# Running the feed-forward part for three groups per block in place of two

## Chip, cores, metric

The kernel runs on one core of a Trainium2 chip. The metric is the device time of one execution in microseconds, lower is better. "Clock" below is the TensorE clock that was granted, as a share of full speed. Times in running text that have no run named are from the instruction times of the profiled execution.

## The reference

For each of 8 batches: squared-relu attention without a softmax, gated by u; then, over all tokens, a feed-forward layer whose hidden unit is the larger of two products.

```python
# u, v: (8, 3072, 256)   z: (8, 3072, 64)
scores = (1/S) * z @ z.T                 # symmetric
attn   = maximum(scores, 0) ** 2
x      = u * (attn @ v)                  # (24576, 256)
g      = maximum(x @ w1, x @ w2)         # d_ff = 1024
out    = g @ w_out                       # fp32
```

## The kernel before

A *group* is 512 query rows: 6 groups a batch, 48 in all, numbered i; g is the number within the batch. A group's attention is 48 *steps* (24 key tiles n, two halves dc of d_model), each a pair of matmuls with 64 rows that run side by side on the two halves of the array.

As the scores are symmetric, a block of scores is made once, by the group that comes first, and turned by DMA transposes on the SyncE queue for the later one. A block *on* the diagonal is its own mirror: in batches 1 to 7 the upper triangle alone is made, and the rest comes from three transposes in place.

```python
def score_pair(b, g, m, ...):            # one pair of score matmuls, relu, square
    ...
    triangle = blk == g and whole_first < (b, g)
    ...                                  # PE: s_ps; ACT: relu -> r_sb; DVE: r*r -> a_sb
    if triangle and m % 2 == 1:
        for j in range(G - 1):
            nc.sync.dma_start_transpose(a[:, j + 1 :, ts(j, P)], a[:, j, (j + 1) * P :])
    if m % 2 == 1 and blk > g:
        if b == 0 and g < 2 and blk > 2:
            later.append((b, g, blk))    # mirrored some steps later
        else:
            mirror(b, g, blk)            # nc.sync.dma_start_transpose -> at_sb
```

`tiles_of` puts the group's own (diagonal) tiles last, n = 20 to 23. Score pairs are made up to 11 ahead of need, at the steps that `pair_slots` lists. Two groups' x wait until a *block*: ff1 (x times w1 - w2, relu) and ff2 (times w_out, plus x times w2 w_out), 128 rows, about 7.8 us of TensorE per group.

```python
def ff_follows(i):
    return i >= 2 and i % 2 == 0 or i == len(groups) - 1
def edge(i):                             # how many last steps are skewed: dc 0 first, then dc 1
    return 0 if ff_follows(i) else 4 if i < 2 else 9
...
for i, (b, g) in enumerate(groups):
    for slot, (n, dc) in enumerate(steps_of(i)):
        ...                              # score pairs, attention step, drain, gate, loads
        if i + 1 < len(groups):
            if i and n == 1:  load_u(*groups[i + 1])     # POOL queue
            if n == 16:       turn_u(*groups[i + 1])     # SyncE queue, transpose
        ...
        if g >= 3 and n in (8, 14) and not late:         # next batch's v, POOL queue
            load_v(b + 1, V_ORDER[2 * (g - 3) + (n == 14)] * G, G)
    now = waiting if ff_follows(i) else []
    g_sbs = [ff(w) for w in now[:1]]
    sums = new or drain(acc, range(KD))
    for j, w in enumerate(now):
        if j: g_sbs.append(ff(w))
        ff2(*w, g_sbs[j])                # o_ps -> ACT copy -> o_sb (2 buffers) -> SyncE queue -> out
```

## Time and profile before

Median 968.79 us (968.57 to 969.14).

| | before |
|---|---|
| span of the profiled execution | 966.4 us |
| TensorE busy, granted clock | 99%, 1.00 |
| DVE, ACT busy | 50%, 58% |
| attention of a group, batches 1 to 7 (first to last attention matmul) | 10.2 to 12.0 us |
| two groups' block with its two ends | 16.3 us |

From the page (busy us and share of the span; the clock's line has 40 equal slices, 9 is 90% or more):

```profile
span 966.4 us, 19478 instructions
...
PE 954.8 (99%) x7994; PEld 621.6 (64%) x8042; DVE 487.2 (50%) x847; ACT 557.6 (58%) x1058; POOL 61.0 (6%) x118
...
PEclk9999999999999999999999999999999999999999
DMA  9999798988689976999869988699967998767611
...
```

There is no slack to see on TensorE. Two small waits of the weight loads (us in total, times, longest) mark a block's ends. They are idle time of the loads; the matmuls themselves start about 0.2 us later per block (0.092 and 0.010 us at the first two of ff1, 0.096 us behind ff2):

```profile
...
PEld L234 <- issue: 9.8, 23, 0.4
...
PEld L147 <- issue: 4.6, 22, 0.2
...
```

### The profile page before, as it was taken

The page shows a single profiled execution, that of the slowest core. Times are in us where ns is not written, and L with a number is a line of the kernel's source. Part 1 is how long each engine was busy: PE and PEld are TensorE (multiplying, and loading weights), DVE is VectorE, ACT ScalarE, POOL GpSimd, SP SyncE. Part 2 cuts the span into 40 slices and gives each one's busy share as a digit, 9 for nine tenths or more (in the row PEclk, how much of TensorE's full clock was granted, in tenths as well). Part 3 has the DMA queues.
Part 4 walks back from the last instruction along what each step waited for, and adds up shares of the span by engine and source line. Part 5 has one row for each costly group of instructions (what it writes and reads, how often), then busy time and mean ns, then how long its engine had stood idle before and what let it go on. Part 6 is the DMA issues. An engine that isn't in the chain of part 4 may idle for free.

```text
span 966.4 us, 19478 instructions
## 1 busy us (share of the span) xinstructions
PE 954.8 (99%) x7994; PEld 621.6 (64%) x8042; DVE 487.2 (50%) x847; ACT 557.6 (58%) x1058; POOL 61.0 (6%) x118
## 2 busy tenths in 40 slices
PE   8999999999999999999999999999999999999998
PEld 4465667675666756667566765676756776566655
DVE  6746454463555534555346553464545554445433
ACT  6757466563575645756456564565556656466433
POOL 3001000100000000000000000000000000000000
PEclk9999999999999999999999999999999999999999
DMA  9999798988689976999869988699967998767611
GB/s 186 186 207 175 135 156 158 179 149 166 134 140 188 146 157 126 164 185 148 150 133 146 184 152 160 131 162 176 150 141 140 157 170 168 135 131 145 124 56 44
DMA packets 382296, 145.99 MB, mean 151 GB/s; under 512 B 360832, under 2 KB 361984, under 8 KB 382208
## 3 DMA queue, kind: packets, MB, share of 16 engines
q1 hardware_dynamic: 365792, 115.25, 62.5%
q0 software_dynamic: 16416, 29.50, 20.8%
q8 instruction: 63, 1.03, 0.4%
q14 instruction: 25, 0.20, 0.1%
HBM read 59.77 MB, written 25.17 MB: 88 GB/s over the span
## 4 chain that ended last, share of the span: by engine, by line
PE 96%; DVE 1%; issue 1%; ACT 1%; DMA 1%; DVEq 0%; POOLq 0%
PE o_ps L263 17%; PE d_ps L234 17%; PE s_ps L147 7%; PE o_ps L255 4%; DMA v_sb<-in_v_dram 1%; DVE a_sb L166 1%; PE acc_12604 L199 1%; PE acc_6354 L199 1%; PE acc_4771 L199 1%; PE acc_3187 L199 1%; PE acc_11103 L199 1%; PE acc_9519 L199 1%; PE acc_7936 L199 1%; PE acc_1582 L199 1%; PE acc_1581 L199 1%
## 5 line engine op out<-in xcount | busy, mean ns | idle before, releaser
L199 PEld LDWEIGHTS <-v_sb 64*128 64x128 bf16 x4608 | 314.6, 94 | 181.4 <-issue 5.9
L160 ACT ACTIVATE r_sb<-s_ps 128x512 bf16<-128x512 f32 (+3 forms) x664 | 333.8, 555 | 90.4 <-PE s_ps L147 88.8
L166 DVE TENSOR_TENSOR a_sb<-r_sb 128x1024 bf16<-128x1024 bf16 x251 | 173.6, 692 | 243.0 <-ACT r_sb L160 239.0
L244 DVE TENSOR_SCALAR g_sb<-d_ps 128x512 bf16<-128x512 f32 x192 | 132.8, 692 | 146.1 <-PE d_ps L234 146.1
L263 PE MATMUL o_ps<-w_out_sb,g_sb 128*128 128x256 bf16 x1536 | 199.1, 273 | 0.0
L234 PE MATMUL d_ps<-xT,w_sb 128*128 128x512 bf16 x720 | 167.4, 379 | 2.6 <-issue 0.2
L263 PEld LDWEIGHTS <-g_sb 128*128 128x128 bf16 x1536 | 150.2, 98 | 20.8
L242 ACT ACTIVATE g_sb<-d_ps 128x512 bf16<-128x512 f32 x192 | 114.8, 598 | 82.0 <-PE d_ps L234 57.1
L147 PE MATMUL s_ps<-zT 64*128 64x512 bf16 (+3 forms) x672 | 148.6, 357 | 0.9 <-DVE r_sb L158 0.5
L270 ACT COPY o_sb<-o_ps 128x512 f32<-128x512 f32 x96 | 56.3, 586 | 150.3 <-PE o_ps L263 149.2
L234 PEld LDWEIGHTS <-w_sb 128*128 128x128 bf16 x768 | 73.2, 98 | 89.6 <-issue 9.8
L255 PE MATMUL o_ps<-W2o_sb,xT 128*128 128x256 bf16 x384 | 73.3, 273 | 0.0
L118 POOL DMA_DIRECT2D un<-in_u_dram x48 | 25.7, 537 | 731.2 <-DMA uT<-un 717.6
L147 PEld LDWEIGHTS <-zT 64*128 64x128 bf16 x672 | 47.6, 94 | 29.0 <-issue 4.6
L220 DVE SCALAR_TENSOR_TENSOR xT<-h_sb,uT 128x512 bf16<-128x512 f32 x96 | 61.8, 685 | 0.0
L164 DVE TENSOR_TENSOR a_sb<-r_sb 128x512 bf16<-128x512 bf16 (+3 forms) x170 | 47.9, 323 | 14.7 <-ACT r_sb L160 14.5
L255 PEld LDWEIGHTS <-xT 128*128 128x128 bf16 x384 | 37.6, 98 | 14.1
L114 POOL DMA_DIRECT2D v_sb<-in_v_dram x48 | 25.8, 546 | 59.1 <-DVE v_sb L113 58.3
L199 PE MATMUL acc_134<-a_sb,v_sb 64*128 64x512 bf16 x24 | 8.7, 377 | 0.5 <-DMA v_sb<-in_v_dram 0.4
L199 PE MATMUL acc_136<-a_sb,v_sb 64*128 64x512 bf16 x24 | 8.7, 378 | 0.0
L199 PE MATMUL acc_137<-a_sb,v_sb 64*128 64x512 bf16 x24 | 8.5, 376 | 0.0
L199 PE MATMUL acc_135<-a_sb,v_sb 64*128 64x512 bf16 x24 | 8.5, 376 | 0.0
(577 smaller groups left out, 1665.3 us busy)
## 6 DMA issues: line engine op xcount, KB each, us to landing
out_dram<-o_sb SPq DMA_DIRECT2D x47, 512.0 KB, 4.0
v_sb<-in_v_dram POOLq DMA_DIRECT2D x48, 256.0 KB, 7.0
un<-in_u_dram POOLq DMA_DIRECT2D x48, 256.0 KB, 5.0
zn<-in_z_dram POOLq DMA_DIRECT2D x7, 384.0 KB, 6.7
a_sb<-a_sb SPq DMA_TRANSPOSE x126, 2.7
at_sb<-a_sb SPq DMA_TRANSPOSE x120, 5.0
uT<-un SPq DMA_TRANSPOSE x48, 3.3
w_132<-in_moe_w_dram POOLq DMA_DIRECT2D x1, 512.0 KB, 5.1
```

The costliest lines, as they stand in the source:

```text
L147: nc.tensor.matmul(s_ps[h][:, lo[h] :], zT[b][rows, 2 * m + h, :], zT[b][rows, g * G + lo[h] // P : g * G + G, :].rearrange("p t c -> p (t ...
L160: nc.scalar.activation(o, s, AF.Relu)
L164: nc.vector.tensor_mul(a[:, k + h, lo[h] :], o, o)
L166: nc.vector.tensor_mul(a[:, k : k + 2, :], r, r)
L199: nc.tensor.matmul(o, v_sb[b][rows, t, ts(dc, P)], mv, start=first, stop=last)
L220: nc.vector.scalar_tensor_tensor(out=xT[:, dc, :].rearrange("p (t r) -> p t r", r=P), in0=hs[dc].rearrange("p (t r) -> p t r", r=P), scala ...
L234: nc.tensor.matmul(d_ps, w15_sb[:, kc, ts(nb, P)], xT[:, kc, :], start=(kc == 0), stop=(kc == KD - 1),)
L242: nc.scalar.activation(g_sb[:, nb, :], d_ps, AF.Relu)
L244: nc.vector.tensor_single_scalar(out=g_sb[:, nb, :], in_=d_ps, scalar=0.0, op=ALU.max)
L255: nc.tensor.matmul(o_ps[:, t, :], xT[:, dc, ts(t0 + t, P)], W2o_sb[:, dc, :], start=(dc == 0), stop=False,)
L263: nc.tensor.matmul(o_ps[:, t, :], g_sb[:, nb, ts(t0 + t, P)], w_out_sb[:, nb, :], start=False, stop=(nb == KF - 1),)
L270: nc.scalar.copy(o_sb[:, t0 : t0 + 2, :], o_ps)
```

## The change

The intent is to switch TensorE between attention and feed-forward less often: 16 blocks in the loop in place of 24. The rest of the diff moves the startup conditions along (the first block is behind group 3) and adapts the score slots.

```diff
     def ff_follows(i):
-        return i >= 2 and i % 2 == 0 or i == len(groups) - 1
+        return i >= 3 and i % 3 == 0 or i == len(groups) - 1
     def edge(i):
-        return 0 if ff_follows(i) else 4 if i < 2 else 9
+        return 0 if ff_follows(i) else 4 if i < 3 else 9
@@ pair_slots
+        if i % 3 == 2:
+            return [3, 9, 14, 19, 24, 29, 41]
@@ main loop
-                    if i < 2:
+                    if i < 3:
                         new[dc] = drain_fast(acc, dc)
-                if i in (1, 2) and n == 10:
+                if i in (1, 2, 3) and n == 10:
-                if i == 2 and n == 16:            # w1 - w2, turn of w2
+                if i == 3 and n == 16:
-            if i == 2:                            # w2 w_out
+            if i == 3:
```

## The prediction

> **What bounds the kernel now.** TensorE. The page has PE busy 954.8 of 966.4 us, clock granted 1.00; in the chain of waits PE holds 96%. In the instruction times, pairs of 64-row matmuls start every 0.216 us, the 512-column d_ps matmuls every 0.216, the 256-column o_ps ones every 0.109. Behind 55 us almost nothing is lost between them except at the ends of an ff block. VectorE is busy 50%, ScalarE 58%. In the first 55 us PE waits for a_sb several times (0.4 to 0.7 us each), as score pairs are needed soon after they are made.
>
> **What a block costs.** Going from attention (64-row tiles) to ff1 (128 rows) the start-to-start distance is 0.09 to 0.11 us above the matmul's own time (up to 0.20 where one row half runs ahead, which is not a cost of the switch), one more 0.01 follows, and from ff2 back to scores it is 0.096 above. The table of waits agrees: PE's weight loads idle before ff1 23 times, before scores 22 times. The Trainium skill, "TensorEngine Tiling (Array Packing)", Key Properties, says that changing the tiling mode drains TensorE; here that is about one exposed weight load (94 to 98 ns) each way, so about 0.205 us per block.
>
> **What the change does.** Ff blocks inside the loop go from 24 to 16 (behind groups 3, 6, ... 45 and 47); no work goes away. Eight blocks fewer: 8 x 0.205 = -1.6 us, all on the critical path. Group 2 of each later batch had its last score pair at slot 26, whose multiply queued behind the two gate operations (2 x 0.685 us on VectorE); the first user waited about 0.09 us. The new slot 24 puts the multiply ahead of the gate: lead 2.37 us against an unqueued latency of 2.36 us (score start to product ready). At most -0.6 us over 7 batches, or nothing. Ends of groups without a block keep the nine-step skew, which shows no wait: 0.
>
> **What it costs.** In group 2 of the first batch the new slots (3, 9, 14, 19, 24, 29, 41) put the last score pair one unit ahead of its first user: lead 0.43 us, latency 2.36, so a PE wait of about 1.9 us near 49 us. The wait of 0.54 us that stood at 50.3 us goes (w2's turn on PE moves to group 3, where leads are 3.4 us or more). The boundary of groups 2 and 3 with four steps of skew: +0.1. The z of the next batch is loaded at group 2, n = 20 (landing took 6.8 us) and doubled on VectorE at group 3, n = 4; a block lay between, now about 5 us: VectorE may wait, mostly hidden by leads: +0.2. Mirrored block (2,3) landed at 54.2, is needed at about 56: no wait. Sum: about +1.7 us.
>
> **Predicted:** -1.6 -0.4 +1.7 gives -0.3; as slots are evidently placed with care, I lean lower: 968.1 us, 8 times in 10 between 966.4 and 970.0. Faster by over 2%: 0.005; within 2%: 0.985; slower: 0.01.
>
> **What would show it.** Right: 16 idle gaps before the first weight load of ff1, not 24, each as long as before; one PE wait for a_sb of 1.7 to 2.2 us at the end of group 2; clock 1.00; busy times of DVE and ACT equal within 1%. Wrong: new PE waits recurring once per batch at the end of group 2 (slot 24 too tight) or group 5, or PE waiting for at_sb transposes or for zd near 55 to 60 us.
>
> **What would make it wrong.** A zn landing later than 58 us, or a transpose queue backing up in groups 2 and 3, whose 16 us of ff cover is gone: +1 to +4 us.

## More of the kernel before

Batch 1, group 2 ends its attention at 172.4 us, the block of two groups lies between, group 3 runs from 188.6 to 200.2 us (start, duration of the issue, line, operation):

```profile
...
164.59 13.59 SPq L181 DMA_TRANSPOSE at_sb<-a_sb  x3
178.27 1.55 SPq L122 DMA_TRANSPOSE uT<-un  x1
179.93 3.76 SPq L169 DMA_TRANSPOSE a_sb<-a_sb  x3
183.79 5.67 SPq L274 DMA_DIRECT2D out_dram<-o_sb  x2
190.84 3.54 SPq L181 DMA_TRANSPOSE at_sb<-a_sb  x1
...
```

The diagonal of group 3 (the three of line 169) is issued at 179.9 to 183.7, and the last of the three lands at 189.4. TensorE asks for the last of them at step n = 23, about 198 us (nine steps and one score pair before the end of the group). It is nearly 9 us early; without the 16.3 us of the block it would be 7 to 8 us late.

## The result

Median 1016.83 us (1013.88 to 1025.83), against 968.79: the ratio is 1.051 (95% interval 1.046 to 1.056). A ratio is the mean time of one kernel's runs over that of the other's of the same rounds, so not quite the ratio of the medians. Executions over 1.5% slower than the fastest of the same kernel are left out of the means. The predicted range ended at 970.0. All five runs have a granted clock of 0.975 to 0.983, where the kernel before has 1.00, and they differ by 1.2%, where those before differ by 0.1%.

```profile
span 1013.7 us, 19464 instructions
...
PE 968.4 (96%) x7994; PEld 630.3 (62%) x8042; DVE 489.7 (48%) x849; ACT 558.2 (55%) x1058; POOL 60.9 (6%) x118
...
PEclk9999999799998999999999899998999999999999
DMA  9996989978679676896848969489794987849611
...
```

The busy time of ACT and DVE is the same to 1% (558.2 and 489.7 us); TensorE has idle slices and slices with a lowered clock, at regular distances. First to last attention matmul of each group tells where (us):

| group in the batch | before, batches 1-7 | after, batches 1 to 7 |
|---|---|---|
| 2 | 11.97 each | 11.55, then 11.65 each |
| 3 | 11.55 each | 19.23, 18.92, 16.20, 18.22, 16.56, 15.55, **11.90** |
| 4 | 11.81 each, last 10.41 | 11.49 each, last 10.30 |
| from the end of group 3 to group 4 (block) | (no block) | 26.57, 25.99, 25.35, 25.72, 26.73, 25.74, **24.05** |
| from the end of group 0 to group 1 (block) | 16.28 each | 24.10 each |

Only group 3 and the block behind it are long, in batches 1 to 6. Batch 7, which has the same instructions but no next batch to load, is not. TensorE at the end of group 3 of batch 1 (start, us, engine, line; in brackets the idle time and what ended it):

```profile
...
186.96 0.38 PE L199 MATMUL acc_2472<-a_sb,v_sb 64*128 64x512 bf16 x1
189.24 0.37 PE L199 MATMUL acc_2471<-a_sb,v_sb 64*128 64x512 bf16 x1 [1.90 <-DMA a_sb<-a_sb]
...
190.50 0.48 PE L199 MATMUL acc_2471<-a_sb,v_sb 64*128 64x512 bf16 x1 [0.66 <-DMA a_sb<-a_sb]
...
195.30 0.58 PE L199 MATMUL acc_2471<-a_sb,v_sb 64*128 64x512 bf16 x1 [3.85 <-DMA a_sb<-a_sb]
...
196.27 0.61 PE L234 MATMUL d_ps<-xT,w_sb 128*128 128x512 bf16 x1
197.10 3.19 PE L234 MATMUL d_ps<-xT,w_sb 128*128 128x512 bf16 x7 [0.22 <-issue]
```

Three waits, each for one of the in-place transposes of the diagonal. The queue shows why, in the same view as that of before:

```profile
...
169.62 14.91 SPq L181 DMA_TRANSPOSE at_sb<-a_sb  x3
184.62 1.26 SPq L122 DMA_TRANSPOSE uT<-un  x1
185.98 4.62 SPq L169 DMA_TRANSPOSE a_sb<-a_sb  x3
190.69 7.69 SPq L96 DMA_TRANSPOSE zT<-zd  x1
...
```

VectorE had made the diagonal long before (two squares of each pair, the last done at 176.3 us):

```profile
...
174.11 0.69 DVE L164 TENSOR_TENSOR a_sb<-r_sb 128x512 bf16<-128x512 bf16 x2
...
175.89 0.42 DVE L164 TENSOR_TENSOR a_sb<-r_sb 128x256 bf16<-128x256 bf16 x2
...
```

So from 176.3 to 186.0 us the transposes did not wait for data: two mirrors and the turn of u stood ahead of them in the queue. Behind the turn of u, the buffer of `un` came free, and the POOL queue sent a load of u and two of v at once:

```profile
...
173.12 0.53 POOL L118 DMA_DIRECT2D un<-in_u_dram  x1 [25.54 <-DMA uT<-un]
173.64 1.07 POOL L114 DMA_DIRECT2D v_sb<-in_v_dram  x2
189.36 0.53 POOL L118 DMA_DIRECT2D un<-in_u_dram  x1 [14.65 <-DMA uT<-un]
189.88 1.08 POOL L114 DMA_DIRECT2D v_sb<-in_v_dram  x2
```

The third transpose, issued at 189.42, landed at 195.26. An earlier burst of the same kind, at 173.1 us, had fallen on the two mirrors ahead: they took 12.0 and 9.8 us from issue to landing, those of batch 7, which loads no v, 8.9 and 5.8. In the transfer records the queue of the loads holds 0.98 and 1.03 of the 16 engines' time from 192 to 196 us, that of the transposes 0.09 and 0.04. The kernel before has the same order and the same burst (its third transpose took from 182.5 to 189.4), but group 3 was then still behind a block.

The cost goes on after the wait, in the windows up to the wait, during it, and over the block (columns: stretch, us, busy of each engine, granted clock, DMA share, GB/s):

```profile
...
core 0: us, PE busy (x) PEld busy (x) DVE busy (x) ACT busy (x) POOL busy (x), PEclk, DMA share, GB/s
176.50:187.00 10.50, 10.50 (x102) 6.58 (x99) 6.47 (x14) 7.60 (x16) 0.00 (x0) 1.00 1.34 172
187.00:195.80 8.80, 2.38 (x15) 0.64 (x12) 1.36 (x2) 1.02 (x2) 1.60 (x3) 0.71 0.77 115
195.80:222.00 26.20, 25.88 (x169) 16.73 (x168) 9.57 (x14) 10.86 (x19) 1.60 (x3) 0.90 0.92 183
...
```

The clock's record falls to half at 190.6 us, between the second and the third wait, and stays there until 200.9 us: ff1 starts with matmuls 0.43 us apart in place of 0.216.

The waits of the weight loads no longer show the block's ends alone: those of ff1 are more, not fewer. The half clock adds them: in f4 below, where the clock stays up in these blocks, they are 15.

```profile
...
PEld L234 <- issue: 22.3, 66, 0.8
...
PEld L147 <- issue: 3.8, 17, 0.5
...
```

The sum over the profiled execution, after against before:

- group 3 of batches 1 to 6 against batch 7's 11.9: 104.7 - 6 x 11.9 = +33.3 us; 
- the blocks behind them against 24.05: 156.1 - 144.3 = +11.8 us; 
- start to group 7: 152.3 - 148.7 = +3.6 us; group 1 of batch 1: +0.7 us;
- the rest is left with about -2 us (the spans differ by 1013.7 - 966.4 = +47.3 us), which is the gain that the change was made for.

### The profile page after: what moved, and what is told of

It is laid out like the page before. It is cut to its first block, busy times and chain, and to the rows that moved or that the text cites. A ratio compares the mean times of both kernels' runs of the same rounds, so it can differ in the third digit from the quotient of the medians.

```text
span 1013.7 us, 19464 instructions
## 1 busy us (share of the span) xinstructions
PE 968.4 (96%) x7994; PEld 630.3 (62%) x8042; DVE 489.7 (48%) x849; ACT 558.2 (55%) x1058; POOL 60.9 (6%) x118
## 3 DMA queue, kind: packets, MB, share of 16 engines
q0 software_dynamic: 16416, 29.50, 19.9%
q8 instruction: 63, 1.03, 0.4%
## 4 chain that ended last, share of the span: by engine, by line
PE 88%; DMA 7%; issue 2%; DVE 2%; ACT 1%; SPq 0%; POOL 0%; DVEq 0%; ACTq 0%; POOLq 0%
PE d_ps L234 17%; PE o_ps L263 16%; PE s_ps L147 6%; PE o_ps L255 4%; DMA a_sb<-a_sb 4%; DMA v_sb<-in_v_dram 2%; DMA at_sb<-a_sb 1%; ACT r_sb L160 1%; DVE a_sb L166 1%; DMA out_dram<-o_sb 1%; PE acc_6269 L199 0%; PE acc_4686 L199 0%; PE acc_3103 L199 0%; PE acc_7853 L199 0%; PE acc_9436 L199 0%
## 5 line engine op out<-in xcount | busy, mean ns | idle before, releaser
L199 PEld LDWEIGHTS <-v_sb 64*128 64x128 bf16 x4608 | 327.0, 94 | 213.4 <-issue 43.8
L166 DVE TENSOR_TENSOR a_sb<-r_sb 128x1024 bf16<-128x1024 bf16 x251 | 173.8, 693 | 186.0 <-ACT r_sb L160 183.6
L234 PE MATMUL d_ps<-xT,w_sb 128*128 128x512 bf16 x720 | 175.7, 395 | 3.5 <-issue 1.3
L147 PE MATMUL s_ps<-zT 64*128 64x512 bf16 (+3 forms) x672 | 163.8, 358 | 1.2 <-DVE r_sb L158 0.5
L234 PEld LDWEIGHTS <-w_sb 128*128 128x128 bf16 x768 | 76.5, 101 | 96.4 <-issue 22.3
L147 PEld LDWEIGHTS <-zT 64*128 64x128 bf16 x672 | 54.6, 94 | 29.2 <-issue 3.8
L164 DVE TENSOR_TENSOR a_sb<-r_sb 128x512 bf16<-128x512 bf16 (+3 forms) x170 | 47.3, 322 | 44.3 <-ACT r_sb L160 43.7
L255 PEld LDWEIGHTS <-xT 128*128 128x128 bf16 x384 | 37.5, 98 | 14.1
L199 PE MATMUL acc_2471<-a_sb,v_sb 64*128 64x512 bf16 x12 | 4.8, 402 | 6.4 <-DMA a_sb<-a_sb 6.4
L199 PE MATMUL acc_4054<-a_sb,v_sb 64*128 64x512 bf16 x12 | 4.7, 393 | 6.5 <-DMA a_sb<-a_sb 6.5
L199 PE MATMUL acc_7220<-a_sb,v_sb 64*128 64x512 bf16 x12 | 4.7, 393 | 5.6 <-DMA a_sb<-a_sb 5.6
L199 PE MATMUL acc_134<-a_sb,v_sb 64*128 64x512 bf16 x24 | 8.7, 377 | 0.6 <-DMA v_sb<-in_v_dram 0.5
```

Source lines behind the costliest of these rows:

```text
L147: nc.tensor.matmul(s_ps[h][:, lo[h] :], zT[b][rows, 2 * m + h, :], zT[b][rows, g * G + lo[h] // P : g * G + G, :].rearrange("p t c -> p (t ...
L164: nc.vector.tensor_mul(a[:, k + h, lo[h] :], o, o)
L166: nc.vector.tensor_mul(a[:, k : k + 2, :], r, r)
L199: nc.tensor.matmul(o, v_sb[b][rows, t, ts(dc, P)], mv, start=first, stop=last)
L234: nc.tensor.matmul(d_ps, w15_sb[:, kc, ts(nb, P)], xT[:, kc, :], start=(kc == 0), stop=(kc == KD - 1),)
L255: nc.tensor.matmul(o_ps[:, t, :], xT[:, dc, ts(t0 + t, P)], W2o_sb[:, dc, :], start=(dc == 0), stop=False,)
```

## The experiments

Theory T after the result: TensorE waits for the in-place transposes of group 3 and then runs at half clock because it idled. They are late because (1) the block that covered them is gone, (2) they stand in the queue behind two mirrors that nobody needs yet, and (3) loads of v and u take the DMA engines just then. Rivals: the mirrors are late and the diagonal is only named last; the scores come late from ACT and DVE; three ff2 in a row and the output buffers hold everything up.

Edits are against the changed kernel unless said otherwise. All nine kernels gave correct results.

### e1: no in-place transposes in group 3

```diff
-        triangle = blk == g and whole_first < (b, g)
+        triangle = blk == g and g != 3 and whole_first < (b, g)
```

> The changed kernel, but group 3 of batches 1 to 7 computes its diagonal block of scores in full, so that the three in-place transposes (a_sb<-a_sb) of that group do not exist. Theory T (PE waits at the end of group 3 for these three transposes, which stand in the SyncE queue behind two mirrors, and then runs ff1 at half clock because it idled): attention of group 3 in batches 1 to 6 falls from 15.6-19.2 us to about 12.1, no stretch with granted clock under 1, time 970 to 975 us. Rival R1 (the mirrors at_sb are late, the triangle is only named last): waits move to at_sb, time stays above 1000. Rival R2 (scores of group 3 come too late from ACT and DVE): more work for both, time the same or longer than 1016.

990.01 us (986.54 to 998.79), ratio 1.023. Group 3 takes 11.84 or 11.85 us in each batch, its block 24.05 us in each: T's two terms are gone and both first rivals with them, although ACT and DVE had more to do. The time is 15 to 20 us above what was expected, though, and the clock still falls in two other places. New waits stand there: group 4 takes 17.8 us in batch 5, with a gap of 3.2 us behind ACT's copy to o_sb, and in batch 1 group 0 takes 18.1 where it took 12.2, with a wait of 4.6 us for v_sb. The next runs show what the first is; the second stays open.

### e2: the two mirrors behind the diagonal

```diff
-            if b == 0 and g < 2 and blk > 2:
+            if b == 0 and g < 2 and blk > 2 or b > 0 and g == 2 and blk > 3:
                 later.append((b, g, blk))
...
-                if later and n % 4 == 0 and (i > 1 or i == 1 and n > 12):
+                if later and n % 4 == 0 and (1 < i < 6 or i == 1 and n > 12 or i > 5 and g == 3):
```

> The changed kernel, with the mirrors of blocks (2,4) and (2,5) of batches 1 to 7 held back until group 3, so that the in-place transposes of group 3 are no longer behind them in the SyncE queue. If the order in the queue is what makes them late (T-order): they land 6 to 10 us earlier, group 3 takes 12 to 13.5 us, time 971 to 980. If the competing loads of v and u alone make them late (T-load): group 3 improves by under 3 us, time above 995.

1003.81 us (993.28 to 1006.71), ratio 1.034. Group 3 takes 11.82 to 11.90 us in batches 1 to 7: the change of order is enough to lose the diagonal's wait. It moves the turn of u forward too, and with it the loads: in batch 1 the first diagonal transpose still took 8.1 us (179.7 to 187.8), but the third landed at 188.8, about 4 us before its need. But the time came out far above the 971 to 980 expected, mostly because group 4 now takes 14.8 to 19.5 us in five of the batches 1 to 6. ACT and TensorE after the block, batch 1:

```profile
...
222.91 1.07 ACT L270 COPY o_sb<-o_ps 128x512 f32<-128x512 f32 x2 [9.78 <-DMA out_dram<-o_sb]
...
```

```profile
...
223.54 0.75 PE L147 MATMUL s_ps<-zT 64*128 64x256 bf16 x2 [4.85 <-ACT o_sb L270]
...
```

ACT waited 9.78 us in front of the third ff2's copy, because o_sb has two buffers and the first output transfer had not landed; the relus of the next scores stand behind that copy, and TensorE waits for a score bank. So there is a second mechanism (O), which the changed kernel mostly hides, perhaps because its block starts later, behind the wait for the diagonal, with fewer transposes left in the queue (argued, not tested). The changed kernel's own table of waits has 8.2 us of it on ACT, in two places.

### e3: the loads of v out of the way

```diff
+    V_HELD = [(4, 2), (4, 8), (4, 14), (5, 2), (5, 8), (5, 14)]
...
-                    if g >= 3 and n in (8, 14) and not late:
-                        load_v(b + 1, V_ORDER[2 * (g - 3) + (n == 14)] * G, G)
+                    if not late and (g, n) in V_HELD:
+                        load_v(b + 1, V_ORDER[V_HELD.index((g, n))] * G, G, held=True)
```

> The changed kernel, with the six v loads of the next batch tied to groups 4 and 5 (in place of groups 3 to 5 and issued as soon as the POOL queue reaches them), so that none runs beside the transposes before the end of group 3. T-load (batch 7, which loads nothing, showed 11.9 us in group 3 with the same order of transposes): group 3 of batches 1 to 6 takes 12 to 13.5 us, time 971 to 980. T-order alone: group 3 stays above 15 us, time above 1005.

981.48 us for the median of three runs (976.35 to 988.66; a fourth, 992.66, was slow), ratio 1.014. With the order of the SyncE queue untouched, group 3 takes 11.9 to 14.1 us, and all blocks behind it 24.05. So the loads of v are necessary too for the long wait, as batch 7 had suggested; up to 2.2 us of it stay in a batch. Most of the gain is in the queue ahead: the third transpose was issued 7.0 us after the start of group 3 in place of 11.0 (mean of batches 1 to 6), but from issue to landing it still took 5.5 us in place of 6.1, beside the load of u, which was not moved. The 971 to 980 expected were missed by the median, if by little; the profiled run (979.7 us span) has 3.9 us of wait for v_sb at the start of batch 1, where loads that the edit does not touch come late.

### e4: blocks of three behind groups 2 and 5

Edited from the kernel before: `ff_follows` is `i % 3 == 2`; the startup and group 2 of batch 0 stay as before; the groups with a block neither in front nor behind (i % 3 == 1, from group 4 on) use the slots 3, 9, 14, 19, 24, 29, 41.

> Three groups per block too, but with the blocks behind groups 2 and 5 of each batch (first block behind group 2 as in the kernel before, startup as before, no group-2 slot 41 in batch 0). T: a block of 24 us now lies between the products of group 3's diagonal and their use, so the wait for a_sb is gone; 8 block ends fewer than before at 0.2 us: 966 to 969 us, provided no other group runs out of cover (group 5 or group 2 would show it). A rival that lays the loss on the length of the blocks itself (three ff2 in a row, out_dram, g_sb) expects 1000 us or more here.

983.82 us (978.80 to 985.43), ratio 1.015. No wait for the diagonal, blocks of 24.10 us: three groups in a row are not what costs 48 us. But the 966 to 969 were missed: group 3, now behind the block, takes 13.0 to 16.5 us in five of the seven batches, with 11.5 us of PE s_ps waiting for ACT o_sb, mechanism O of e2.

### f1: e2 with a third o_sb buffer

```diff
 (e2, and)
-    tpool = ...(name="tpool", bufs=13)          # at_sb: pays for the space
+    tpool = ...(name="tpool", bufs=12)
-    opool = ...(name="opool", bufs=2)
+    opool = ...(name="opool", bufs=3)
+        if i == 2:                              # slots of before, in batch 0 alone
+            return [3, 9, 15, 21, 26, 31, 36, 40]
```

> e2 (mirrors of (2,4) and (2,5) after the in-place transposes) with a third buffer for o_sb (paid for by one at_sb buffer, 13 to 12) and, in group 2 of batch 0 alone, the score slots of the kernel before. Theory O (with three ff2 in a row the third o_sb copy on ACT waits for the first output transfer, which stands behind transposes; the scores' relus queue behind that copy, and PE waits for s_ps at the start of group 4): the waits PE s_ps <- ACT o_sb vanish, group 4 takes 11.5 to 12 us in all batches in place of 14.8 to 19.5, time 972 to 980. The wait for a_sb of 1.84 us near 49.5 us in group 2 of batch 0 falls under 0.6. If instead group 4 waits for something that the late mirrors bring (at_sb): group 4 stays above 14 us and the wait names at_sb.

966.78 us (966.50 to 971.33), ratio 0.998 (0.996 to 0.999), below the 972 to 980 expected. From group 7 on TensorE has no wait left but the block ends: from batch 1 on group 3 takes 11.90 us in each batch, group 3's block 24.05, and group 4 11.49 (10.30 in the last). The wait before block ends, in the same table as that of before:

```profile
...
PEld L234 <- issue: 6.4, 15, 0.4
...
PEld L147 <- issue: 3.6, 17, 0.2
...
```

15 in place of 23, and from group 7 to the end 815.5 us in place of 817.7. The waits in group 2 of batch 0 near 48 and 50 us (0.71 and 1.84 us in the changed kernel) are 0.28 each with the old slots, under the 0.6 expected; a wait of 0.67 us now stands at 51.8 us, at the border to group 3, where the accumulators are handed over (h_sb). The profiled run is the slowest of the five (971.33): batch 0's group 3 takes 17.6 us and waits 2.7 us for an at_sb mirror, so the startup remains weaker than that of before.

### f2: e4 with a third o_sb buffer

The same pool edit on e4.

> e4 (blocks behind groups 2 and 5) with a third buffer for o_sb (at_sb 13 to 12). Theory O: group 3 of batches 1 to 6 falls from 13.0-16.5 to 11.6 us, all waits at block ends gone: 966 to 968.5 us, just under the kernel before, as eight block ends of 0.2 us are saved. If the third buffer only moves the wait elsewhere: above 972.

967.93 us (966.92 to 974.53), ratio 1.001 (0.997 to 1.005): within the 966 to 968.5 expected, but the gain over the kernel before that this range implied isn't shown. Group 3 takes 11.55 us in batches 1 to 7; O is the cause of e4's loss. As a block lies in front of group 3, this needs no change of the queue's order; 0.8 us of wait for diagonals is left in group 2 of batches 1 and 2.

### f3: a third o_sb buffer alone

The same pool edit on the changed kernel, nothing else.

> The changed kernel with a third buffer for o_sb (at_sb 13 to 12) and nothing else. Theory T (the in-place transposes of group 3 are the main loss of the changed kernel): nothing much changes, group 3 of batches 1 to 6 stays at 15 to 19 us, time 1008 to 1020. Rival: the output buffers are the root (they hold the SyncE queue up and with it the transposes): time falls under 990.

1025.95 us (1023.84 to 1035.60), ratio 1.061. Group 3 takes 16.8 to 18.4 us in batches 1 to 6 and 11.9 in batch 7. The output buffers are not the root; the extra loss against 1016.83 lies in the startup of the profiled run (9.2 us of wait for v_sb in batch 1, 7.8 us for a mirror in batch 0, which has one at_sb buffer fewer). The time is above the range.

### f4: TensorE kept busy during the wait

```diff
+                if g == 3 and 0 < b < B - 1 and n == 20 and dc == 0:
+                    fill = mm_psum.tile([P, GW], fp32, name="fill", tag="mm")
+                    for _ in range(20):
+                        nc.tensor.matmul(fill, warm[:, :P], warm, start=True, stop=True)
                 attn_unit(b, g, tiles_of(b, g)[n], acc, dc, n == 0, n == NT - 1)
```

> The changed kernel, with 20 matmuls of 512 columns that nothing reads (about 4.3 us) ahead of the first diagonal step of group 3 in batches 1 to 6, so that PE works during most of the wait. Theory C (about 1 to 2.7 us per batch of the loss is not the wait but ff1 and the last steps run at half clock after the idle time): group 3 keeps its length (+0 to +1 us where the wait was short), the granted clock is above 0.995, the ff block behind it takes 24.1 us in each batch in place of 25.3 to 26.7, time 1002 to 1010. If the clock falls for another reason than idling: clock stays near 0.98 and time is 1016 or more.

```profile
...
core 0: 1010.3 us, clock 0.996
...
```

(The changed kernel's own profiled run: 0.981.) Group 3 keeps its length (16.4 to 18.5 us, 105.1 us over batches 1 to 6 against 104.7, with 4.5 us of each spent in work that nobody reads), the clock is 0.996, and the block behind takes 24.05 us in every batch. So the 11.8 us in these blocks are the half clock, and it comes from idling. From group 7 to the end f4's profile takes 850.3 us, the changed kernel's 861.3. The time itself, 1014.34 us for the median of three runs (1012.25 to 1014.99; a fourth, 1027.62, was slow), is above the 1002 to 1010 expected: in the profiled run group 0 of batch 1 took 19.9 us, with a wait of 6.5 us for v_sb. It is 3.9 us in e3's profile and 9.2 in f3's, while in that of the changed kernel group 0 of batch 1 is only 0.3 us longer than in the next batches: how late batch 1's v arrives differs from kernel to kernel. I did not settle what sets it.

### g1: the version that beats both

From the kernel before: two-group blocks behind groups 2, 4 and 6 as before, then three-group blocks behind 9, 12, ... 45 and 47, with e2's queue order from batch 1 on, f1's pools, and the slots 3, 9, 14, ... 41 where i > 6 and i % 3 == 2.

> The startup of the kernel before (blocks of two groups behind groups 2, 4 and 6), then blocks of three behind group 9, 12, ... 45 and 47, with the mirrors of (2,4) and (2,5) held back and a third o_sb buffer as in f1. From group 7 to the end f1's profile took 815.5 us and that of the kernel before 817.7, so this should be about 2.2 us under the kernel before, 966 to 967.5 us, without f1's run with a slow startup (971). If the block ends were worth nothing it would be equal to the kernel before, 968.5 to 969.5.

966.05 us (965.80 to 969.36), ratio 0.997 (0.996 to 0.999), 3.0 us under the 969.07 us of the kernel before in the same chip's runs, and within the 966 to 967.5 expected. It is a gain of 0.3%, clear of the noise but small.

```profile
span 964.2 us, 19453 instructions
...
PE 953.2 (99%) x7994; PEld 622.9 (65%) x8042; DVE 488.0 (51%) x847; ACT 558.7 (58%) x1058; POOL 61.2 (6%) x118
...
PEclk9999999999999999999999999999999999999999
...
```

## Why the prediction was wrong

**Right.** What bounds the kernel and what a block's two ends cost: about 0.2 us together, with 15 or 16 such gaps left in the mended kernels. The Trainium skill's sentence on mode switches, cited in the prediction ("TensorEngine Tiling (Array Packing)", Key Properties), has no figure; the 0.092 us into ff1 and 0.096 us back, wherever the clock is full, are in keeping with it. The expected gain of about 2 us exists (f1: 2.2 us from group 7 on). The new wait in group 2 of batch 0 was 1.84 us where 1.9 was predicted, and f1 with the old slots takes most of it away. ACT and DVE busy times are equal within 1%.

**The step that failed:** "Ends of groups without a block keep the nine-step skew, which shows no wait: 0." It looked at the accumulators' hand-over alone. Taking a block away from behind group 2 takes away the 16.3 us of matmuls under which the transposes of group 3 travelled. The leads were counted from the score to the finished square (2.36 us), which is where most blocks of scores end; a diagonal block ends with three more transposes, and here those were issued 9.7 us after the square. The check of the transpose queue ("Mirrored block (2,3) landed at 54.2, is needed at about 56") was made in batch 0, which has no in-place transposes. One look at landing against need in a later batch (189.4 against 198, with 16.3 us of block between) would have shown a deficit of 7 to 8 us, or about 6 without the skew at the end of group 3; 3.7 to 7.3 were measured.

**A named risk that was mis-sized.** "A transpose queue backing up in groups 2 and 3, whose 16 us of ff cover is gone: +1 to +4 us." This is what happened, but it happens once in each of batches 1 to 6. It measured +33.3 us of waits, 3.7 to 7.3 us in each of six batches; and behind it +11.8 us of half clock, which the prediction did not have at all.

**The clock.** The Trainium skill, "TensorE: Matmul & The Clock Gate", Why this matters for your kernels, warns against TensorE-idle gaps over about 3 us, after which the clock halves. The trace agrees in kind, but less idling was enough: the matmuls at 190.50 us are already slow (0.48 to 0.63 us against 0.38) after idle times of 1.90 and 0.66 us with four matmuls between. f4 shows that filling the time removes it.

**Contention.** The Trainium skill, "DMA: Bandwidth & Descriptors", Queues, rings and completion order, says that each DMA engine goes round the queues a packet at a time. It follows that a load on another queue slows a transpose even though it is not ahead of it. The trace agrees in kind: records of the loads are of about 1.8 KB, of the transposes about 0.25 KB, and the loads had over 0.95 of the engines' time, though from 192 to 194 us the two queues moved nearly as many records (159 and 141). e3 and batch 7 show what it costs, more through the mirrors ahead in the queue than through the diagonal's own transposes.

**What removes the loss.** For the wait in group 3: not having the transposes (e1), their place in the queue (e2), fewer loads beside them (e3, most of it) or a block in front (e4). Each removes all or most of the wait, so none alone is "the" cause; the change lost the slack that had hidden all of them. The output buffers (O) do nothing for that wait (f3), and become the next limit once it is gone (e2 and e4 against f1 and f2).

**Open.** What decides how late v comes for batch 1 and the mirrors in batch 0; g1, which keeps the old startup, shows neither wait. Whether this or the wait in group 3 moves the changed kernel's runs between 1013.9 and 1025.8 us is not shown either, as one run alone has a trace.

## What to carry to other kernels

A phase in which one engine computes something else is cover for every transfer that runs under it; before removing or regrouping such phases, list for each transfer when it lands and when it is needed, in a steady-state stretch and not at startup only, and follow each dependency to its last hop. A queue that issues in order makes a transfer late through what stands ahead of it (here 9.7 us), so put what is needed first, first. When one stall is mended, expect the next limit (here two output buffers for three outputs) before judging the idea.

## What the Trainium skill lacked or had wrong

- "TensorE: Matmul & The Clock Gate", in the table row that is cited above, warns of idle gaps over about 3 us. Here less was enough: the clock halved after two gaps of 1.90 and 0.66 us with four matmuls between them, and at single gaps of 2.59 (e2), 2.69 and 2.92 (e4) and 2.71 us (f1). Gaps of 2.85 and 2.70 us (e2) left it up, so no sharp limit comes out of these runs.
- "DMA: Bandwidth & Descriptors" has the round-robin between queues, but not how uneven it gets: with loads in records of about 1.8 KB beside transposes in records of about 0.25 KB, the loads held 0.98 to 1.03 of the engines' time and the transposes 0.04 to 0.09; an in-place transpose that lands in 2.3 us (median) took 5.84.
- No page of the skill that was read counts the cost of switching between 64-row and 128-row matmuls, which "TensorEngine Tiling (Array Packing)" only says to drain TensorE: 0.092 and 0.010 us at the first two matmuls of ff1, 0.096 back.
